# Attention and a gated feed-forward block on one core: the first load of z in rows of four tokens, and a partial-sum copy moved from ScalarE to VectorE

## The chip, the cores and the metric

The kernel runs on one core of a Trainium2 chip. The metric is the device time of one execution in microseconds (us). Before the change the median of six runs is 1193.26 us, from 1192.84 to 1195.26.

## What is computed

The reference, cut to what matters (B = 8 batches, S = 3008 tokens, D = 256, d_qk = 64, d_ff = 2048):

```python
scores = (1.0 / S) * np.matmul(z, z.transpose(0, 2, 1))   # z: [8, 3008, 64]
attn = np.maximum(scores, 0.0) ** 2
x = (u * np.matmul(attn, v)).reshape(B * S, D)            # u, v: [8, 3008, 256]
h = x @ w_in                                              # w_in: [256, 2048]
out = (h * np.cos(h)) @ w_out                             # w_out: [2048, 256]
```

## The kernel before the change, in words

The tokens of a batch are cut into six columns of up to 512 tokens (the last has 448), and each column, one "slot" s of 48, goes through two phases. The first makes the attention output of the column: scores (z times z, line 194), a ReLU on ScalarE that moves them out of PSUM (line 204), a square on VectorE that leaves a piece A in SBUF (lines 209 and 212), and products of the pieces with v that are added up in PSUM (line 258). The second phase takes the column through the feed-forward block: h (line 404), the cosine on ScalarE (line 412), the product g on VectorE (line 415), and the products with w_out (lines 482 and 525). Everything is issued in an order written out by hand, and each engine runs its own list in order.

**The first columns.** Slots 0, 1 and 2 go through `phase_a_first` one after the other, before any whole second phase. Each output half dh (128 of the 256 columns of the output) is added up in two PSUM banks, one for the upper and one for the lower 64 rows of each block of tokens; the two products of a block run side by side on the two halves of TensorE's rows. One half uses the pair of banks M, the other the two banks of one of the E buffers; in slot 1 the roles are swapped. While a slot's products run, the scores of later groups are issued between them into the other E buffers.

**The end of a first column.** At line 379 `gate_sum` is called for both halves. In each, line 269 copies the first bank to an SBUF tile `sm` on ScalarE, and line 270 adds the second bank to it on VectorE. Then `hold` lets GpSimd read one element of the first sum, which keeps the load of the next u (GpSimd's queue) behind it. After slots 1 and 2 units of the second phase follow (their g at line 415 stands behind the sums on VectorE). PSUM banks come free for the next slot when they have been copied or added.

**The start.** z of batch 0 comes in six transfers at lines 633 and 639, issued in turn on SyncE's and ScalarE's queues. Partition p of transfer g receives the tokens p, p+128, p+256 and p+384 of column g: four rows of 64 float32 (256 bytes) that lie 128 tokens apart in memory. A cast (line 645) makes them float16, and four TensorE transposes per column (line 649) put them into PSUM with the four blocks of 128 tokens side by side; `copy_turned` (line 657 on ScalarE for column 0, line 659 on VectorE for columns 1 to 5) copies them to the tile zT, whose column index is the token. Seven matmuls on zeros (line 664) and four more (line 687) keep TensorE busy before and between the first scores.

Of the kernel before, what the change touches and what calls it, by code (L numbers as in the profile page):

```python
# [14 lines left out]
def kernel(  # L15
# [9 lines left out]
    nc = tc.nc  # L25
# [6 lines left out]
    P = 128  # L32
    H = P // 2
    CW = 512
    NB = (S + P - 1) // P
    NC = (S + CW - 1) // CW
# [10 lines left out]
    def width(J):  # L47
        return CW if J < NC - 1 else WL
# [27 lines left out]
    turned = [ppool.tile([P, CW], FP16, name=f"turned{i}", tag=f"M{i % 2}") for i in range(3)]  # L76
# [17 lines left out]
    def drop_piece(key):  # L94
        i = pieces.pop(key)
        if pending.get(i):
            pending[i] = "dropped"
        else:
            free_pieces.append(i)
# [9 lines left out]
    z16s, zTs, vs, u16s, uTs, xs, gs = {}, {}, {}, {}, {}, {}, {}  # L109
# [48 lines left out]
    def turn_u(s):  # L158
        t = upool.tile([P, 8, P], FP16, name="uT")
        nc.sync.dma_start_transpose(t, u16s.pop(s).rearrange("p j d -> p (j d)"))  # L160
        uTs[s] = t
# [20 lines left out]
    def emit_score(later=None):  # L182
        b, J, I, h = groups[done_groups[0]]
        done_groups[0] += 1
        cut = I == J and not (b == 0 and J < 3)
        W = 2 * P if cut and h == 0 else width(J)
        zT = zTs[b]
        e = E[take_e()]
        for t in range(2):
            k = 4 * I + 2 * h + t  # L190
            half = t if h == 0 else 1 - t
            rows = slice(half * H, (half + 1) * H)
            Wt = min(W, (2 * h + t + 1) * P) if cut else W
            nc.tensor.matmul(  # L194
                e[:, t, 0:Wt],
                zT[rows, k * P:(k + 1) * P],
                zT[rows, J * CW:J * CW + Wt],
                start=True,
                stop=True,
            )  # L200
        key = (b, J, I)
        a = new_piece(key) if h == 0 else piece(key)
        r = rpool.tile([P, 2, CW], FP16, name="r")
        nc.scalar.activation(r[:, :, 0:W], e[:, :, 0:W], AF.Relu)  # L204
        def square():
            if I > J:
                a4 = a.rearrange("p (k t j) -> p t k j", k=4, j=P)[:, 2 * h:2 * h + 2, :, :]
                r4 = r.rearrange("p t (k j) -> p t k j", j=P)
                nc.vector.tensor_tensor(a4, r4, r4, ALU.mult)  # L209
            else:  # L210
                a4 = a.rearrange("p (k w) -> p k w", w=CW)[:, 2 * h:2 * h + 2, 0:W]
                nc.vector.tensor_tensor(a4, r[:, :, 0:W], r[:, :, 0:W], ALU.mult)  # L212

        if later is None:
            square()
        else:
            later.append(square)
        if h == 0:
            return
        if cut or (I > J and (b, J, I) not in direct):  # L220
            turns.append(((b, I), key))
            turns.sort(key=lambda t: t[0])
            turn_slots[key] = pieces[key]
            pending[pieces[key]] = "held"

    def emit_turns(due, more=0):
        while turns and (turns[0][0] <= due or more > 0):
            if turns[0][0] > due:
                more -= 1
            (b, c), key = turns.pop(0)  # L230
            b, J, I = key
            i = turn_slots[key]
            a = piece_bufs[i]
            if I == J:
                a4 = a.rearrange("p (k w) -> p k w", w=CW)
                for rr in range(1, 4):
                    rows = P if J * 4 + rr < NB - 1 else H
                    nc.sync.dma_start_transpose(
                        a4[:, 0:rr, rr * P:rr * P + rows],
                        a[0:rows, rr * CW:rr * CW + rr * P],  # L240
                    )
            else:
                d = new_piece((b, I, J))
                nc.sync.dma_start_transpose(d.rearrange("p (n j) -> p n j", j=P), a)
            if pending.pop(i) == "dropped":
                free_pieces.append(i)
# [10 lines left out]
    def emit_value(b, J, k, t, dh, bank, start, stop):  # L257
        nc.tensor.matmul(  # L258
            bank[:, 0:width(J)],
            vs[b, k // 4][t * H:(t + 1) * H, k % 4, dh * P:(dh + 1) * P],  # L260
            value_rhs(b, J, k, t),
            start=start,
            stop=stop,
        )

    def gate_sum(s, b0, b1):
        W = width(s % NC)
        sm = spool.tile([P, CW], FP32, name="sm")
        nc.scalar.copy(sm[:, 0:W], b0[:, 0:W])
        nc.vector.tensor_tensor(sm[:, 0:W], b1[:, 0:W], sm[:, 0:W], ALU.add)  # L270
        return sm

    def gate_mul(s, dh, sm, eng=None):
        eng = eng or nc.vector
        J = s % NC
        b = s // NC
        W = width(J)
        if s not in xs:
            if J == NC - 1 and b % 2 == 1:
                xs[s] = xodd  # L280
            else:
                xs[s] = xpool.tile([P, 2, CW], FP16, name="x")
        x = xs[s]
        uT = uTs[s].rearrange("p (k d) j -> p k d j", d=2)
        nk = W // P
        eng.tensor_tensor(  # L286
            x[:, dh, 0:nk * P].rearrange("p (k j) -> p k j", j=P),
            sm[:, 0:nk * P].rearrange("p (k j) -> p k j", j=P),
            uT[:, 0:nk, dh, :],
            ALU.mult,  # L290
        )
        if nk < 4:
            dst = x[:, dh, nk * P:W] if b % 2 == 1 else xodd[:, dh, W:CW]
            eng.tensor_tensor(
                dst, sm[:, nk * P:W], uT[:, nk, dh, 0:W - nk * P], ALU.mult
            )
# [44 lines left out]
    late_sums = []  # L341
    mix_at = {9: ("s2", 0), 19: ("s2", 1), 29: ("s4", 0), 35: ("s4", 1)}

    def hold(src):
        nc.gpsimd.tensor_copy(mark[:, 0:1], src)

    def phase_a_first(s, n, extra={}):
        b, J = s // NC, s % NC
        ea = e_order.pop(0)
        pair = [E[ea][:, 0, :], E[ea][:, 1, :]]  # L350
        acc = [pair, M] if s == 1 else [M, pair]
        last = NB - 1
        run = 1 if s == 0 else 2
        steps = [
            (dh, k)
            for I in range(0, NC, run)
            for dh in range(2)
            for k in range(4 * I, min(4 * (I + run), last))
        ] + [(2, last)]
        lo, hi = 5 if s == 0 else 2, 42  # L360
        at = {}
        for i in range(n):
            p = lo + (hi - lo) * i // (n - 1)
            at[p] = at.get(p, 0) + 1
        for i, (dh, k) in enumerate(steps):
            if i in extra:
                extra[i]()
            if dh == 2:
                emit_value(b, J, last, 0, 0, acc[0][0], False, True)
                emit_value(b, J, last, 1, 1, acc[1][1], False, True)  # L370
            else:
                for t in range(2):
                    emit_value(
                        b, J, k, t, dh, acc[dh][t], k == 0, k == last - 1 and t != dh
                    )
            if dh > 0 and (k % 4 == 3):
                drop_piece((b, J, k // 4))
                if s > 0:
                    emit_turns((0, 0), 1)
                    if k < 4:  # L380
                        turn_u(s)
                    elif k < 8:
                        for d in range(2):
                            gate_mul(s - 1, d, late_sums.pop(0))
            for _ in range(at.get(i, 0)):
                emit_score(later=squares if s == 0 and i == lo else None)
        if s == 0:
            turn_u(0)
        late_sums.extend(gate_sum(s, *acc[dh]) for dh in range(2))
        hold(late_sums[0][0:1, 0:1])  # L390
        load_u(s + 1)
        e_order.append(ea)
# [237 lines left out]
    for g in range(NC):  # L630
        eng = nc.sync if g % 2 == 0 else nc.scalar
        full = 4 if g < NC - 1 else 3
        eng.dma_start(
            z32[g][:, 0:full, :],
            z[0, g * CW:g * CW + full * P, :].rearrange("(j p) d -> p j d", p=P),
        )
        if full == 3:
            for r in range(2):
                nc.sync.dma_start(z32[g][r * H:(r + 1) * H, 3, :], z[0, S - H:S, :])
# [12 lines left out]
            )  # L652

    def copy_turned(g):
        dst = zTs[0][:, g * CW:(g + 1) * CW]
        if g == 0:
            nc.scalar.copy(dst, turned[g])
        else:
            nc.vector.tensor_copy(dst, turned[g])

    wc = cpool.tile([P, 2, CW], FP16, name="c")
    nc.scalar.activation(wc[:, 0, 0:P], warm[:, 0:P], AF.Sin)
# [118 lines left out]
```

## Time and profile before

| | before |
|---|---|
| median of six runs | 1193.26 us |
| the profiled execution's own time | 1193.04 us |
| its span, first to last instruction | 1191.3 us |
| TensorE busy in the span | 1183.5 us (99%) |
| VectorE busy | 1012.2 us (85%) |
| ScalarE busy | 794.4 us (67%) |
| sum copies on ScalarE, line 269, slots 0 to 2 | 6, of 582 to 606 ns |
| sum adds on VectorE, line 270, slots 0 to 2 | 6, of 681 to 686 ns |
| copy of turned z, column 0, ScalarE, line 657 | 0.585 us |
| copies of turned z, columns 1 to 5, VectorE, line 659 | 0.41 to 0.42 us each |
| the z transfers of 128 KB, issue to landing | 3.7 us median on SyncE's queue, 3.9 on ScalarE's |

The times in the profile are microseconds from the span's start. In a list of instructions by time a line has the start, the length, the engine (PE is TensorE's matmul, DVE VectorE, ACT ScalarE, POOL GpSimd, SP SyncE), the line of the kernel, the operation, and the shapes of output and input. Instructions of one engine overlap by a little, so the distance of two starts is the time that one takes from its engine, and is shorter than its length. The chain of waits follows the work that ended last back to the start: its lines have a start, a length, and the engine and line on which the time was spent.

### The profile page before, as it was taken

The page shows a single profiled execution, that of the slowest core. Times are in us where ns is not written, and L with a number is a line of the kernel's source. Part 1 is how long each engine was busy: PE and PEld are TensorE (multiplying, and loading weights), DVE is VectorE, ACT ScalarE, POOL GpSimd, SP SyncE. Part 2 cuts the span into 40 slices and gives each one's busy share as a digit, 9 for nine tenths or more (in the row PEclk, how much of TensorE's full clock was granted, in tenths as well). Part 3 has the DMA queues.
Part 4 walks back from the last instruction along what each step waited for, and adds up shares of the span by engine and source line. Part 5 has one row for each costly group of instructions (what it writes and reads, how often), then busy time and mean ns, then how long its engine had stood idle before and what let it go on. Part 6 is the DMA issues. An engine that isn't in the chain of part 4 may idle for free.

```text
span 1191.3 us, 29044 instructions
## 1 busy us (share of the span) xinstructions
PE 1183.5 (99%) x11887; PEld 726.3 (61%) x11887; DVE 1012.2 (85%) x1302; ACT 794.4 (67%) x927; POOL 689.1 (58%) x717
## 2 busy tenths in 40 slices
PE   9999999999999999999999999999999999999998
PEld 4566665665566656666566665656666566665566
DVE  6888888889988898888988889888888888888776
ACT  7966676667666676667676676666766666666454
POOL 3286746657466573755647556476565665545452
PEclk9999999999999999999999999999999999999999
DMA  9999998569995699945999459974898839954301
GB/s 160 173 176 156 126 158 131 102 122 139 138 131 97 123 141 162 131 84 104 158 149 131 86 105 162 170 117 71 123 164 148 122 72 126 178 110 86 65 20 54
DMA packets 479862, 148.00 MB, mean 124 GB/s; under 512 B 404208, under 2 KB 479472, under 8 KB 479728
## 3 DMA queue, kind: packets, MB, share of 16 engines
q1 hardware_dynamic: 380752, 112.93, 53.9%
q0 software_dynamic: 97440, 32.78, 26.9%
q8 instruction: 93, 1.52, 0.5%
q10 hardware_dynamic: 1536, 0.43, 0.2%
q14 instruction: 41, 0.34, 0.1%
HBM read 66.32 MB, written 24.64 MB: 76 GB/s over the span
## 4 chain that ended last, share of the span: by engine, by line
PE 97%; ACT 1%; DVE 1%; issue 0%; DMA 0%; POOL 0%; DVEq 0%; ACTq 0%
PE E L404 27%; PE M L482 23%; PE M L258 20%; PE E L258 19%; PE E L194 5%; PE M L525 1%; ACT r L204 1%; PE M L460 1%; DVE g L415 0%; DMA z<-in_z_dram 0%; DVE sm L270 0%; PE E L525 0%; POOL s L433 0%; ACT c L412 0%; DVE A L212 0%
## 5 line engine op out<-in xcount | busy, mean ns | idle before, releaser
L412 ACT ACTIVATE c<-E 128x1024 f16<-128x1024 f32 (+1 forms) x384 | 385.3, 1006 | 216.6 <-PE E L404 214.4
L415 DVE SCALAR_TENSOR_TENSOR g<-E,c 128x1024 f16<-128x1024 f32 (+1 forms) x384 | 458.9, 1197 | 61.6 <-ACT c L412 60.6
L204 ACT ACTIVATE r<-E 128x512 f16<-128x512 f32 (+1 forms) x342 | 327.8, 966 | 112.2 <-PE E L194 106.7
L258 PEld LDWEIGHTS <-v 64*128 64x128 f16 x4512 | 245.3, 94 | 230.0 <-issue 17.5
L404 PE MATMUL E<-x,w_in 128*128 128x512 f16 (+1 forms) x1408 | 354.0, 375 | 0.0
L433 POOL TENSOR_TENSOR s<-g 128x512 f16<-128x512 f16 (+1 forms) x184 | 207.6, 1128 | 189.6 <-DVE g L415 139.6
L258 PE MATMUL M<-A,v 64*128 64x512 f16 (+1 forms) x2256 | 283.0, 372 | 0.0
L258 PE MATMUL E<-A,v 64*128 64x512 f16 (+1 forms) x2256 | 278.0, 372 | 0.0
L434 POOL TENSOR_TENSOR g<-g 128x512 f16<-128x512 f16 (+1 forms) x184 | 218.7, 1188 | 14.4
L404 PEld LDWEIGHTS <-w_in 128*128 128x128 f16 x1536 | 133.1, 98 | 108.9 <-issue 19.5
L482 PEld LDWEIGHTS <-g 128*128 128x128 f16 x2816 | 172.5, 98 | 40.8
L209 DVE TENSOR_TENSOR A<-r 128x1024 f16<-128x1024 f16 x240 | 173.3, 734 | 15.1 <-ACT r L204 14.3
L286 POOL TENSOR_TENSOR x<-sm,uT 128x512 f16<-128x512 f32 (+1 forms) x43 | 48.6, 1131 | 213.6 <-DVE sm L270 213.2
L482 PEld LDWEIGHTS <-s 128*128 128x128 f16 x2112 | 129.4, 98 | 32.1 <-DVE s L440 0.5
L194 PE MATMUL E<-zT 64*128 64x512 f16 (+4 forms) x684 | 127.5, 355 | 1.8 <-DVE sm L270 0.7
L440 DVE TENSOR_TENSOR s<-s,g 128x1024 f16<-128x1024 f16 (+1 forms) x92 | 99.7, 1085 | 2.1 <-POOL s L433 2.1
L482 PE MATMUL M<-w_mix,s 128*128 128x128 f16 x1408 | 94.0, 219 | 0.3 <-POOL s L433 0.3
L482 PE MATMUL M<-w_mix,g 128*128 128x128 f16 x1408 | 93.6, 219 | 0.0
L482 PE MATMUL M<-w_out,g 128*128 128x128 f16 x1408 | 93.6, 219 | 0.0
L212 DVE TENSOR_TENSOR A<-r 128x512 f16<-128x512 f16 (+1 forms) x102 | 80.7, 792 | 8.6 <-ACT r L204 7.9
L194 PEld LDWEIGHTS <-zT 64*128 64x128 f16 x684 | 38.7, 94 | 38.6 <-issue 4.0
L442 DVE TENSOR_TENSOR s<-g,s 128x1024 f16<-128x1024 f16 (+1 forms) x92 | 60.6, 662 | 0.0
(58 smaller groups left out, 647.3 us busy)
## 6 DMA issues: line engine op xcount, KB each, us to landing
out_dram<-o SPq DMA_DIRECT2D x87, 256.0 KB, 2.1
v<-in_v_dram POOLq DMA_DIRECT2D x40, 256.0 KB, 8.8
u<-in_u_dram POOLq DMA_DIRECT2D x40, 256.0 KB, 4.8
A<-A SPq DMA_TRANSPOSE x252, 5.1
z<-in_z_dram POOLq DMA_DIRECT2D x14, 192.0 KB, 10.6
z<-in_z_dram POOLq DMA_DIRECT2D x14, 176.0 KB, 6.0
v<-in_v_dram POOLq DMA_DIRECT2D x8, 192.0 KB, 11.9
u<-in_u_dram POOLq DMA_DIRECT2D x8, 192.0 KB, 3.9
```

Of the source, the lines that this page charges most:

```text
L194: nc.tensor.matmul(e[:, t, 0:Wt], zT[rows, k * P:(k + 1) * P], zT[rows, J * CW:J * CW + Wt], start=True, stop=True,)
L204: nc.scalar.activation(r[:, :, 0:W], e[:, :, 0:W], AF.Relu)
L209: nc.vector.tensor_tensor(a4, r4, r4, ALU.mult)
L212: nc.vector.tensor_tensor(a4, r[:, :, 0:W], r[:, :, 0:W], ALU.mult)
L258: nc.tensor.matmul(bank[:, 0:width(J)], vs[b, k // 4][t * H:(t + 1) * H, k % 4, dh * P:(dh + 1) * P], value_rhs(b, J, k, t), start=start, ...
L404: nc.tensor.matmul(e[:, f, 0:W], w_in16[:, k, ft * P:(ft + 1) * P], x[:, k, 0:W], start=(k == 0), stop=(k == 1),)
L412: nc.scalar.activation(c[:, :, 0:W], e[:, :, 0:W], AF.Sin, bias=half_pi, scale=inv_s2)
L415: return lambda: nc.vector.scalar_tensor_tensor(gs[m][:, 2 * i:2 * i + 2, 0:W], e[:, :, 0:W], 1.0, c[:, :, 0:W], ALU.mult, ALU.mult)
L433: nc.gpsimd.tensor_tensor(s1[:, f, 0:n], g[:, f, low], g[:, lower, low], ALU.add)
L434: nc.gpsimd.tensor_tensor(g[:, f, low], g[:, f, up], g[:, f, low], ALU.subtract)
L440: nc.vector.tensor_tensor(s2[:, f, 0:n], s1[:, f, 0:n], g[:, f, up], ALU.subtract)
L482: nc.tensor.matmul(acc[:, k * P:(k + 1) * P], left[:, ft, k * P:(k + 1) * P], right[:, ft, :], start=(ft == 0 and k == 0), stop=(ft == F - ...
```

## The change

Two things are changed. First, partition p of a z transfer now receives four tokens that follow one another (4p to 4p+3 of the column, 1024 bytes in one piece) for columns 0 to 4; the transposes then leave block j holding the tokens 4p+j, and the copy to zT writes each of its 512 elements four elements apart from the last, which puts the tokens in order again. Column 5, which is not full, is left as it was. Second, in slots 0, 1 and 2 the copy of the first bank for the first half (dh = 0) is done by VectorE instead of ScalarE. The copy of the second half stays on ScalarE, as do all copies of later slots. VectorE's list then has, at the end of each of these slots: the last squares, the copy, the two adds, and (after slots 1 and 2) the products g. The lists of the other engines keep their order, with one copy fewer on ScalarE.

```diff
-    def gate_sum(s, b0, b1):
+    def gate_sum(s, b0, b1, by=None):
         W = width(s % NC)
         sm = spool.tile([P, CW], FP32, name="sm")
-        nc.scalar.copy(sm[:, 0:W], b0[:, 0:W])
+        (by or nc.scalar.copy)(sm[:, 0:W], b0[:, 0:W])
         nc.vector.tensor_tensor(sm[:, 0:W], b1[:, 0:W], sm[:, 0:W], ALU.add)
         return sm
...
-        late_sums.extend(gate_sum(s, *acc[dh]) for dh in range(2))
+        late_sums.extend(
+            gate_sum(s, *acc[dh], by=(nc.vector.tensor_copy, nc.scalar.copy)[dh]) for dh in range(2)
+        )
         hold(late_sums[0][0:1, 0:1])
...
         eng.dma_start(
             z32[g][:, 0:full, :],
-            z[0, g * CW:g * CW + full * P, :].rearrange("(j p) d -> p j d", p=P),
+            z[0, g * CW:g * CW + full * P, :].rearrange(
+                "(p j) d -> p j d" if full == 4 else "(j p) d -> p j d", p=P
+            ),
         )
...
     def copy_turned(g):
-        dst = zTs[0][:, g * CW:(g + 1) * CW]
+        dst, src = zTs[0][:, g * CW:(g + 1) * CW], turned[g]
+        if g < NC - 1:
+            dst = dst.rearrange("q (p j) -> q j p", j=4)
+            src = src.rearrange("q (j p) -> q j p", j=4)
         if g == 0:
-            nc.scalar.copy(dst, turned[g])
+            nc.scalar.copy(dst, src)
         else:
-            nc.vector.tensor_copy(dst, turned[g])
+            nc.vector.tensor_copy(dst, src)
```

## The prediction

> **What bounds the kernel now.** I read the page first (busy time and the shares of the chain), then the busy time by stage, then the chain of waits over the first 60 us, then the single instructions around it. The page's lines on engines and chain:
>
> ```profile
> PE 1183.5 (99%) x11887; PEld 726.3 (61%) x11887; DVE 1012.2 (85%) x1302; ACT 794.4 (67%) x927; POOL 689.1 (58%) x717
> PE 97%; ACT 1%; DVE 1%; issue 0%; DMA 0%; POOL 0%; DVEq 0%; ACTq 0%
> ```
>
> TensorE sets the time. Where it stands idle is seen by stage (length, then busy time and count of PE, PEld, DVE, ACT, POOL):
>
> ```profile
> 5.00:10.00 5.00, 4.56 (x37) 1.88 (x34) 3.96 (x8) 4.36 (x5) 3.58 (x6) 1.00 0.97 132
> 20.00:25.00 5.00, 4.45 (x42) 2.21 (x39) 3.95 (x7) 5.00 (x7) 0.42 (x2) 1.00 1.15 194
> 35.00:40.00 5.00, 4.55 (x30) 1.67 (x28) 4.28 (x7) 4.47 (x6) 1.57 (x3) 1.00 1.18 216
> 50.00:55.00 5.00, 5.00 (x40) 3.02 (x37) 4.10 (x7) 5.00 (x8) 0.18 (x1) 1.00 1.42 190
> 100.00:200.00 100.00, 100.00 (x1016) 59.60 (x1012) 87.31 (x116) 70.10 (x83) 58.81 (x65) 1.00 0.92 138
> ```
>
> All idle time that the change could touch lies before 45 us: at the start, at the end of slot 0 (24 us) and of slot 1 (38 to 41 us). After that TensorE has no gap until the last 41 us, which the change doesn't touch, so a delay or gain in the first 60 us should reach the end unchanged. The chain of waits shows what TensorE waits for:
>
> ```profile
> 0.74 3.19 DMA z<-in_z_dram
> 3.95 0.44 DVE z L645
> 4.43 0.62 PE turned L649 x4
> 5.08 0.59 ACT zT L657
> 5.72 0.41 PE E L194 x2
> ...
> 23.17 0.69 DVE A L212
> 23.86 1.21 DVE sm L270 x2
> 25.11 0.39 PE E L194 x2
> ...
> 37.35 0.40 DVE sm L270
> 37.95 0.68 DVE sm L270
> 38.63 2.37 DVE g L415 x2
> 41.04 0.39 PE E L194 x2
> ```
>
> At both slot ends VectorE is the chain: its last square, two adds, and after slot 1 two products g. ScalarE's copies (line 269) are not on it.
>
> **The sum copies, slot 0.** VectorE's list by time: square at 23.17, add of M at 23.78, add of E at 24.38 (0.68 long, so done at 25.06). The score at 25.11 writes the E buffer that this last add reads. ScalarE's copy of M ran from 23.03 to 23.61, ready before the square was through, so VectorE went from one instruction to the next, 0.60 to 0.61 apart. The change puts one more instruction between the square and the first add. Everything behind it moves by what it takes: the second add, the score, the square at 25.06. ScalarE gets its copy of E 0.47 earlier, but the add of E is now held by VectorE.
>
> What does a VectorE copy of 128x512 float32 from PSUM to SBUF take? No row of before shows it. From below: the copies of turned z (0.42 for 512 float16 from PSUM) and the cast at line 645 (0.43 for 512 float32 from SBUF); less the overlap of 0.08 that the adds show, 0.34. From above: the add of line 270, which also reads 512 float32 from PSUM and writes float32, 0.68 long and 0.60 apart. The other VectorE rows that read float32 from PSUM agree with it on the cost of a column: line 495 takes 0.425 for 256, line 415 takes 1.20 for 1024, and with 0.68 for 512 that is 1.0 ns for each added column. I take the add's **0.60**. Slot 0: +0.60 (bounds +0.34 and +0.60).
>
> The Trainium skill, "VectorE: DVE Perf Modes" (section "Why PSUM operands drop a tier"), says that a PSUM operand leaves VectorE one read port, and float32 from it one element per cycle; its table of cycles gives (120 + 512) / 0.96 GHz = 0.66 us as an estimate. That speaks against moving this copy to VectorE; by it the sum below would be the same within 0.1, while the two-elements rows would make it about half.
>
> **Slot 1.** Here dh = 0 is the E buffer. Square at 36.74, adds at 37.35 and 37.95, then g at 38.63 twice. ScalarE's copy ended at 37.18, so again only VectorE holds the first add. One copy more moves both adds and both g by 0.60. TensorE waits for these: for M's second bank at 38.65, for g at 39.91 and again at 41.04. Between them it has idle time of its own, but each waiting point moves by the same 0.60, so +0.60 (bounds 0.34 and 0.60). ScalarE's cosines come up to 0.1 earlier; their g wait on VectorE anyway.
>
> **Slot 2.** VectorE here:
>
> ```profile
> 53.22 0.69 DVE L209 TENSOR_TENSOR A<-r 128x1024 f16<-128x1024 f16 x1 [0.23 <-ACT r L204]
> 53.82 0.69 DVE L270 TENSOR_TENSOR sm<-M,sm 128x512 f32<-128x512 f32 x1
> 54.42 0.68 DVE L270 TENSOR_TENSOR sm<-E,sm 128x512 f32<-128x512 f32 x1
> 55.11 2.35 DVE L415 SCALAR_TENSOR_TENSOR g<-E,c 128x1024 f16<-128x1024 f32 x2
> ```
>
> TensorE has eight matmuls of line 404 until 54.65 as cover, then line 525 writes M from 54.66; the third of these (0.11 apart, so 54.88) needs M's second bank, which the add freed at 54.51. With the copy it is free at 55.11: 0.23 late, with the semaphore some 0.25. The next unit at 55.53 (then 55.78) needs the E buffer, freed by the second add at 55.70: covered. The g go from 55.11 to 55.71; the E buffers they free are next written at 57.27 and 58.1, by then freed at about 56.9 and 58.1. So **+0.25** (bounds 0, as the cheap copy ends at 54.85, and 0.60, if the g chain binds).
>
> `hold` reads the first sum, which comes 0.60 later; so does the load of the next u on GpSimd's queue and, behind it, the transpose of u and five transposes of A on SyncE's. All of TensorE's work has moved as much, and the transposes issued at 31.35 lie before 50 us and serve slot 3 and later. Cost nothing; without that cover it would be at most the same 0.60.
>
> **The start.** Column 0's way is: landing at 3.95, cast 0.44, transposes at 4.43, copy on ScalarE from 5.08 to 5.66, score at 5.72. TensorE's seven zero matmuls start 0.43 apart from 1.19, so the last ends at 1.19 + 7 x 0.43 = 4.2. If z lands earlier, the transposes can start at 4.2, not before: the gain is at most 0.25. Does it land that much earlier? Between 2.5 and 3.9 us the queues moved 280 to 290 GB/s at 99% busy in rows of 256 bytes. Stores in rows of 1024 bytes landed 1.7 us after issue for 128 KB and 2.1 for 256 KB, against 3.2 for this load; nothing says more than that it lies between no gain and 1.5. A quarter of a us is near the low end, so I take **-0.20** (bounds 0 and -0.25).
>
> The Trainium skill, "DMA: Bandwidth & Descriptors" (section "Why small descriptors are slow"), gives 11 cycles for a 256-byte piece where 8 carry data; four such in one piece would then need some 35 instead of 44, an estimate of 0.2 us less for the 256 KB of the first two columns. No run here shows that yet.
>
> The copies now write every fourth element. Column 0's on ScalarE lies on the chain: no row shows a stepped write; ScalarE takes 1.02 for 1024 columns against 0.585 for 512, 0.85 ns a column; unchanged from below, twice the column cost (+0.44) from above. I take unchanged, being nearest to the row of the same engine. On VectorE 0.42 may become 0.68. Column 1's copy ends at 5.93 and is read at 7.24 (cover 1.3); column 2's delays squares read at 8.79 (cover 0.7); column 3's ends at 9.16 and delays squares read from 11.6; column 4's ends at 10.98, 0.7 before the next VectorE instruction. Cost nothing; without cover 0.26 each. Column 5's copy at 11.71, which TensorE waits for at 12.19, is the old one.
>
> **Sum.** -0.20 + 0.60 + 0.60 + 0.25 = **+1.25 us**. The profiled execution took 1193.04 (span 1191.3 and 1.74 around it), so 1194.29; the median of the runs is 0.22 above it, so 1194.5. That is 0.10%, and about 0.2% (2.4 us) is what a measurement of this kernel can tell from no change.
>
> **Rivals.**
> 1. *The copy is cheap* (0.34): slots give 0.34 + 0.34 + 0, less 0.20 is +0.5, 1193.8. For it: 0.42 rows of VectorE. Against: none of them reads float32 from PSUM.
> 2. *The start gives nothing back*: z lands no earlier and the stepped copy on ScalarE is twice as dear a column: +0.44 + 1.45 = +1.9, 1195.2. For it: no stepped row. A milder form is that TensorE's slow first rate (128-column transposes 0.107 apart until 5.16, full rate at 5.72) catches the earlier scores.
> 3. *TensorE falls back to its slow rate.* At the start matmuls of 512 columns come 0.43 apart, later 0.216, after some 4 us of work. If idle time at the end of slot 1 brings the slow rate back for as long, half of 4.2 us is lost: +2.1 + 1.25 = +3.3, 1196.6, slower by 0.28%. It decides from the point where half idle is enough: between 38.2 and 41.3 TensorE idles about 1.2 us and keeps full rate; the change makes it 1.8 of 3.7. Against: that it holds now at about 40%.
> 4. *ScalarE was the hidden bound*: it loses three copies 0.48 apart, -1.45, with the start -1.65, 1191.6. For it: ScalarE busy 5.00 of 5 at the end of slot 0. Against: the chain, where each add starts as VectorE comes free and not as a copy ends.
>
> **Chances and range.** Forecast 0.56, rival 1 0.16, rival 2 0.13, rival 3 0.07, rival 4 0.08. The unknowns' bounds give 0.68 - 0.25 = +0.4 to 1.8 + 0.44 = +2.2, so 1193.7 to 1195.5; with 0.4 either way for the median (four of the six runs lie within 0.42 of theirs) 1193.3 to 1195.9, which leaves out rivals 3 and 4. Faster by over 0.2% 0.01 (TensorE's idle time from 5 to 45 us is only 1.8), within 0.2% 0.91, slower 0.08 (rival 3 and a little of rival 2).
>
> **What would show it.** In the changed profile: z's first cast before 3.95 and transposes near 4.2; line 657 still near 0.59; a line 269 row on VectorE of 0.66 to 0.69; the score at the start of slot 1 0.4 later (0.60 - 0.20), TensorE's wait at 41.04 about 1.0 later, line 525's first about 1.0 later with a gap after two matmuls. A copy of 0.42 makes it rival 1; 512-column matmuls 0.43 apart near 41 us make it rival 3; a sum that starts earlier than before makes it rival 4.

## The result, and the profile after

The change makes the kernel slower: 1197.26 us median (16 runs) against 1193.28 (36 runs) beside it, 4.0 us more, a ratio of 1.0032 with a 95% interval from 1.0025 to 1.0038. The profiled execution took 1197.02 us, its span is 1195.2. The forecast was +1.25 us, with a range up to 1195.9.

Of the page of the changed kernel, the same two lines that the prediction shows of before:

```profile
PE 1183.8 (99%) x11887; PEld 726.7 (61%) x11887; DVE 1016.8 (85%) x1305; ACT 793.9 (66%) x924; POOL 688.8 (58%) x717
PE 96%; DVE 2%; ACT 1%; issue 1%; POOL 0%; ACTq 0%; DVEq 0%
```

TensorE's work is nearly the same (1183.5 us before), the span is 3.9 longer, so 3.6 us of the loss are idle time of TensorE. VectorE's share of the chain went from 1% to 2%. Busy time by stage (length, then PE, PEld, DVE, ACT, POOL) says where:

```profile
5.00:10.00 5.00, 3.70 (x28) 1.41 (x28) 4.16 (x5) 4.51 (x5) 3.31 (x6) 1.00 0.77 102
10.00:15.00 5.00, 3.46 (x32) 1.54 (x31) 4.46 (x6) 1.64 (x3) 4.26 (x7) 1.00 1.13 138
25.00:30.00 5.00, 3.61 (x36) 1.78 (x33) 3.69 (x7) 3.31 (x5) 0.97 (x2) 1.00 0.69 136
40.00:45.00 5.00, 3.83 (x24) 1.36 (x24) 4.56 (x7) 3.08 (x4) 2.07 (x3) 1.00 1.08 190
100.00:200.00 100.00, 100.00 (x1011) 59.89 (x1011) 86.99 (x116) 69.03 (x82) 58.07 (x63) 1.00 0.93 145
```

Before, the second of these rows was:

```profile
10.00:15.00 5.00, 4.81 (x46) 2.23 (x45) 3.11 (x6) 3.40 (x4) 4.79 (x7) 1.00 0.98 120
```

From 5 to 15 TensorE idles for 2.8 us, against 0.6 before (0.44 and 0.19), where the forecast had a gain. Around the ends of slots 0 and 1, from 20 to 30 and from 35 to 45, it idles for 1.4 and 1.2 us, against 0.7 and 0.5. The chain of waits of the changed kernel names the instructions (start, length, engine, line):

```profile
4.36 0.44 PE turned L653 x4
4.82 1.30 ACT zT L664
...
6.17 0.60 PE E L194 x4
6.78 0.34 PE turned L653 x4
7.14 1.30 DVE zT L666
8.44 1.48 DVE A L212 x2
9.92 1.20 DVE zT L666
11.12 1.11 DVE A L209 x2
12.23 1.22 DVE zT L666
...
14.39 0.41 PE E L194 x2
...
25.37 0.69 DVE A L212
26.06 0.61 DVE sm L269
...
26.70 1.30 DVE sm L270 x2
...
28.04 0.39 PE E L194 x2
```

Column 0's copy on ScalarE now takes 1.29 and not 0.59, and the copies of columns 1 to 4 on VectorE 1.28 to 1.30 and not 0.42. VectorE's copies and squares carry the chain from 7.1 to 13.4; before, only column 5's copy was on it here. Two groups of transposes, those of columns 4 and 5, waited for VectorE's copies (in brackets, TensorE's idle time and what ended it):

```profile
11.17 0.38 PE L653 MATMUL turned_e<-id,z 128*128 128x128 f16 x4 [0.59 <-DVE zT L666]
13.49 0.38 PE L653 MATMUL turned_e<-id,z 128*128 128x128 f16 x4 [0.75 <-DVE zT L666]
```

At the end of slot 0 the new copy (26.06) stands between the square and the two adds, as foreseen.

Four points of the order stand in both profiles, and their shift from before to after splits the loss: the score behind column 5's copy from 12.19 to 14.39 (+2.20); the first score held at the end of slot 0 from 25.11 to 28.04 (+2.93, so 0.73 for this end); the score behind the second g of slot 1 from 41.04 to 44.60 (+3.56, 0.63 for this end); the second unit of line 404 after slot 2 from 55.69 to 59.66 in the chain (+3.97, 0.41 for this end). The lines of before for the first and the last point:

```profile
11.71 0.43 DVE zT L659
12.19 0.41 PE E L194 x2
...
55.69 0.86 PE E L404 x4
```

The lines after for the third and the last point:

```profile
44.60 0.41 PE E L194 x2
...
59.66 0.86 PE E L406 x4
```

Single profiles scatter here: in four other profiles of kernels whose start is that of before, the score that is at 12.19 came at 11.82 to 12.45. So the first of the four parts is known to some 0.3 us.

### The profile page after: what moved, and what is told of

Same layout as the page of the kernel before. It is cut to its first block, busy times and chain, and to the rows that moved or that the text cites. A ratio compares the mean times of both kernels' runs of the same rounds, so it can differ in the third digit from the quotient of the medians.

```text
span 1195.2 us, 29043 instructions
## 1 busy us (share of the span) xinstructions
PE 1183.8 (99%) x11887; PEld 726.7 (61%) x11887; DVE 1016.8 (85%) x1305; ACT 793.9 (66%) x924; POOL 688.8 (58%) x717
## 4 chain that ended last, share of the span: by engine, by line
PE 96%; DVE 2%; ACT 1%; issue 1%; POOL 0%; ACTq 0%; DVEq 0%
PE E L406 27%; PE M L484 23%; PE M L258 20%; PE E L258 19%; PE E L194 5%; ACT r L204 1%; PE M L527 1%; PE M L462 1%; DVE zT L666 0%; DVE g L417 0%; DVE A L212 0%; PE E L671 0%; DVE A L209 0%; DVE sm L270 0%; DVE sm L269 0%
## 5 line engine op out<-in xcount | busy, mean ns | idle before, releaser
L436 POOL TENSOR_TENSOR g<-g 128x512 f16<-128x512 f16 (+1 forms) x184 | 218.7, 1189 | 14.4
L209 DVE TENSOR_TENSOR A<-r 128x1024 f16<-128x1024 f16 x240 | 173.1, 734 | 15.1 <-ACT r L204 14.4
```

Source lines behind the costliest of these rows:

```text
L436: nc.gpsimd.tensor_tensor(g[:, f, low], g[:, f, up], g[:, f, low], ALU.subtract)
```

## The experiments

The theory after the result: the stepped writes make the copies of turned z slow and cost the start 2.2 us; the sum copies cost 1.8 at the three slot ends. Rivals: the sum copies carry most of it; the copies are slow for another reason (the faster loads, or any step in the pattern); part of the loss is a wait for a load. Each run is compared with the kernel before, run beside it.

**The first part alone.** Its edit is the change without its pieces in `gate_sum` and in the call at line 379.

> The first part of the change alone: z in rows of four tokens and the copies that write every fourth element; all six sum copies on ScalarE as before. Theory: the stepped copy takes 1.3 us on either engine (0.585 on ScalarE and 0.42 on VectorE before) and costs the start 2.2 us, so about +2.2 us, 1195.5, with the score of slot 0 that waited at 12.19 coming at 14.4. Rival, that the sum copies carry most of the 4 us: this run within 0.5 us of before.

Measured: 1195.20 us against 1193.65, ratio 1.0015 (1.0006 to 1.0023). The medians differ by 1.55 us, the ratio gives 1.8, somewhat less than the 2.2 expected. The score behind column 5's copy came at 14.11 (expected 14.4), 1.9 later than before, and that shift was still 1.9 to 2.0 in slots 1 and 2. The copies took 1.28 to 1.30. The rival falls.

**The second part alone.**

> The second part alone: the first half's sum copied by VectorE, z loaded and copied as before. Theory: VectorE's copy takes 0.68 and the add behind it does not overlap it, since it reads what the copy wrote, so 0.72 at the ends of slots 0 and 1 and 0.3 to 0.45 at slot 2: +1.5 to +1.9 us, 1194.8 to 1195.2. Rival (the parts are not independent, the late start makes the slot ends dearer): under +1.0 us.

Measured: 1195.41 against 1193.65, ratio 1.0014 (1.0005 to 1.0023): +1.76, as expected, though its profile also has a wait of 0.5 us at line 527 for the load of w_out, so a part of this may be that load. The parts cost about the same.

**Rows of four, not put in order.** The copy stays as it was:

```diff
-            z[0, g * CW:g * CW + full * P, :].rearrange("(j p) d -> p j d", p=P),
+            z[0, g * CW:g * CW + full * P, :].rearrange(
+                "(p j) d -> p j d" if full == 4 else "(j p) d -> p j d", p=P
+            ),
```

> z in rows of four tokens, but plain copies as before and sum copies on ScalarE: it leaves out the putting in order, so the first batch's tokens in zT stand in another order. Theory (the stepped write alone makes the copies slow): copies at 0.585 and 0.42, first cast at 3.6, transposes from 4.15, first score at 5.45, 0.2 to 0.3 us below before: 1193.0. Rival (the faster loads get in the way of the copies): copies near 1.3 us and about +2.2 us, as in the run of the first part alone.

The copies took 0.59 and 0.42, the first cast started at 3.56, the transposes at 4.15, the first score at 5.46, and the score behind column 5's copy at 11.93: the step alone makes the copies slow, not the loads. But the time was 1194.19 against 1193.65, and the ratio of the runs 0.9999 (0.9990 to 1.0008), an interval that holds the quotient of the two medians too: no gain is seen at the end, where 1193.0 was expected. In this profile TensorE waited 1.3 us at line 525 for the load of w_out, a wait that the profile of before doesn't show.

**The order put in by the read.** The copies read PSUM in steps of 256 bytes and write without a gap:

```diff
...
+        if g < NC - 1:
+            dst = dst.rearrange("q (p j) -> q p j", j=4)
+            src = src.rearrange("q (j p) -> q p j", j=4)
...
```

> z in rows of four tokens, put in order by copies that read PSUM in steps of 256 bytes and write zT without a gap; sum copies on ScalarE; the result is the reference's. Theory (what costs is the stepped write to SBUF): ScalarE's copy unchanged at 0.585, VectorE's at most 0.7, so 0.2 to 0.3 us below before, 1193.0. Rival (any step between 2-byte elements costs, in reading too): copies near 1.3 us, about +2.2 us.

ScalarE's copy took 0.59, VectorE's 0.69 and 0.68 (0.42 without a step). The score behind column 5 came at 11.80, 0.39 earlier than before. The median was 1193.41 against 1193.65, ratio 1.0000 (0.9992 to 1.0009), with runs from 1192.48 to 1195.69. The slowest was the profiled one, and TensorE's list of waits in it begins:

```profile
PE M L525 <- DMA w_out<-in_moe_w_out_dram: 2.6, 1, 2.6
```

w_out's load was issued at 38.96 and landed 18.0 later, against 14.4 before, where TensorE needed it 0.9 us after it had landed (39.35 + 14.4 = 53.75, line 525 at 54.66). The load was issued 0.39 earlier than before, as much as the score came earlier, so the earlier start took nothing of this margin; the slower landing used it up (16.7 in the run with rows of four not put in order). Why it landed later is not shown. It needs no faster start: the run with the copies behind the end, further below, is the kernel before up to there, and it waited 0.2 us at line 525 with a landing of 15.7.

**Rows of two**, copies that write every second element.

> z in rows of two tokens (512 bytes), put in order by copies that write every second element; sum copies on ScalarE; the result is the reference's. If each 2-byte element written by itself costs the same whatever lies between: copies near 1.3 us and about +1.5 to 2 us, as with every fourth. Rival, if the cost grows with the distance covered (1024 columns of zT instead of 2048): copies near 0.7 to 0.9 us and under +0.7 us.

Copies of 0.73 to 0.74 on both engines, so the cost of a copy grows with the distance. The time was 1194.47 against 1193.57, ratio 1.0006 (0.9997 to 1.0015): whether it stays under the +0.7 us that was expected for this case can't be told. The profile has a wait of 0.4 us for w_out.

**The cost of the stepped write by itself.** Copies behind the last store's computation:

```diff
+    for eng in (nc.vector.tensor_copy, nc.scalar.copy):
+        for src in (flat[:, 0:CW], E[1][:, 0, :]):
+            for step in (1, 2, 4):
+                eng(wide[:, 0:CW * step].rearrange("p (n s) -> p n s", s=step)[:, :, 0], src)
...
```

> The kernel before with 24 copies appended behind the last store's computation, on VectorE and then on ScalarE: 512 columns of float16 from SBUF and of float32 from PSUM to float16 with one, two and four elements' distance between written elements, then 128 columns of float32 from PSUM to float32 and to float16 with the same distances. Its total time is not compared. If the cost is one of 2-byte elements written alone: the float16 rows rise to about 1.3 us at distance 2 and 4 alike and the float32 rows don't rise. If it is one of the distance in bytes: float16 at distance 4 (8 bytes) is like float32 at distance 2 (8 bytes), and float16 at 2 lies between. If the stepped write only hurts beside the other work of the start: no row rises above 0.75 us.

From PSUM to float16, 512 columns, at distances 1, 2 and 4, VectorE and then ScalarE:

```profile
1183.82 0.69 DVE L756 CAST A<-E 128x512 f16<-128x512 f32 x1
1184.55 0.73 DVE L756 CAST A<-E 128x512 f16<-128x512 f32 x1
1185.32 1.30 DVE L756 CAST A<-E 128x512 f16<-128x512 f32 x1
```

```profile
1193.10 0.59 ACT L756 CAST A<-E 128x512 f16<-128x512 f32 x1
1193.72 0.73 ACT L756 CAST A<-E 128x512 f16<-128x512 f32 x1
1194.48 1.29 ACT L756 CAST A<-E 128x512 f16<-128x512 f32 x1
```

Only the distance of the written elements differs between the rows of one engine, and the engines agree at 2 and 4, so it is the write that decides there. These copies lie at the end of the kernel, so the other work of its start is not to blame. With 128 columns distance 4 took 0.44 on both, so a further column costs (1.30 - 0.44) / 384 = 2.2 ns, and at distance 2 (0.73 - 0.30) / 384 = 1.1 ns. Neither of the two rules that I had written down holds: distances 2 and 4 are not alike, and it is not the distance in bytes, since 128 columns at 8 bytes took 0.44 as float16 and 0.29 (VectorE) as float32. From SBUF, VectorE took 0.28, 0.46 and 0.74, ScalarE 0.62, 0.76 and 1.32. Why VectorE is cheaper from SBUF, and what the mechanism is, stays open.

**An early load of w_out**, on the kernel before and on the one with the stepped read:

```diff
+    nc.gpsimd.dma_start(w_out16, moe_w_out.rearrange("(k p) f -> p k f", p=P))
     phase_a_first(1, 12)
-    nc.gpsimd.dma_start(w_out16, moe_w_out.rearrange("(k p) f -> p k f", p=P))
```

> The kernel before with one change: the load of w_out is issued behind slot 0 instead of slot 1, some 14 us earlier. In the runs with the faster start TensorE waited 1.3 and 2.6 us for this load at line 525. Theory (the load's landing decides the runs above the fastest ones, and takes back what a faster start gains): the wait is gone, the median 0.3 to 0.7 us below before and the runs closer together. Rival (the load, issued earlier, delays u and the transposes): no gain, or a new wait behind a transfer before 60 us.

> Rows of four put in order by stepped reads of PSUM, and w_out's load issued behind slot 0; the result is the reference's. Theory: the start's gain of 0.3 to 0.4 us is no longer lost to the wait for w_out and adds to that of the early load: 0.7 to 1.0 us below before. Rival (something else is late next, a v load or the transposes of u): no better than the early load alone.

The first took 1193.21 (1192.76 to 1193.77) against 1193.57 (1192.80 to 1195.88), ratio 0.9995 (0.9986 to 1.0004); the second 1192.93 (1192.53 to 1193.55), ratio 0.9994 (0.9985 to 1.0003). The issue moved to 25.80 and 25.07, and neither profile has a wait for w_out. The runs lie closer together, as expected, but both gains are within the intervals: a version that beats the kernel before is not shown. Between these two medians the stepped read's start is worth 0.28 us, with runs that overlap.

**The parts once more without the blur of that load.** Column 0 alone with the stepped write (columns 1 to 4 read in steps), then columns 1 to 4 alone. The edit of the first, against the stepped read with the early load:

```diff
-            dst = dst.rearrange("q (p j) -> q p j", j=4)
-            src = src.rearrange("q (j p) -> q p j", j=4)
+            order = "q j p" if g == 0 else "q p j"
+            dst = dst.rearrange("q (p j) -> " + order, j=4)
+            src = src.rearrange("q (j p) -> " + order, j=4)
```

> As the kernel with stepped reads and the early load of w_out (1192.9), but column 0's copy on ScalarE writes every fourth element as in the change; columns 1 to 4 keep the stepped read. Theory (this copy lies on the chain and nothing hides it): +0.7 us, its added length, so 1193.6. Rival (the late copies of VectorE alone carry the loss): within 0.2 us of 1192.9.

The median is 1194.25, 1.3 above 1192.93 and not 0.7 (ratio to the kernel before 1.0007, 0.9998 to 1.0017). But five of the ten runs lie from 1193.22 to 1193.72, five from 1194.79 to 1195.27. The lower five are where the theory put them, +0.6 at their middle (1193.52). The profiled run, 1195.18, is of the upper five, and its chain shows what happened:

```profile
4.36 0.44 PE turned L651 x4
4.82 1.30 ACT zT L663
...
6.17 1.03 PE E L194 x3
7.20 0.54 PE turned L651 x4
```

The transposes at 4.36 are 0.11 apart, TensorE's slow rate. It then idled for 0.96 us behind the copy, and the four score matmuls at 6.17 took 1.03, against 0.61 at 5.72 before: the slow rate was still on, and matmuls came at half speed until about 10 us. The profile's column of granted clock reads 1.00 all the while, so the rate is read from the matmuls' distances alone. The longer idle time does not settle it: in the profiles of the change and of its first part alone TensorE idled the same 0.96 us, and the scores at 6.17 took 0.60; with the early load of w_out alone it idled 0.25, and the scores at 5.59 took 1.03, with the full rate from 6.56. What decides how long the slow rate lasts stays open. That it also made the other four runs of the upper group long is an inference from their times.

> The other way round: column 0 with the stepped read, columns 1 to 4 on VectorE with the stepped write. Theory (two of TensorE's transposes wait for VectorE's copies, 0.6 and 0.75 us in the run of the first part alone, plus 0.1 for a late square): +1.3 to +1.5 us, 1194.2 to 1194.4. Rival (the copies are covered, as the prediction had it): within 0.2 us of 1192.9.

Measured 1194.46 (1194.21 to 1195.22) and ratio 1.0007 (0.9997 to 1.0016) to the kernel before; 1.5 us above 1192.93. Its chain is VectorE from 5.25 to 12.38, and the transposes of columns 4 and 5 waited 0.55 and 0.75 for VectorE's copies, so the prediction's cover did not hold.

> The second part of the change alone, on the kernel with the early load of w_out (1193.2), so that the load's landing doesn't blur it. Theory (0.72 + 0.63 + 0.41 at the three slot ends): +1.6 to +1.9 us, 1194.8 to 1195.1. Rival, the prediction's size: +1.45 us, 1194.7, or less.

Measured 1194.81 (1194.64 to 1195.04), 1.60 above 1193.21; ratio 1.0009 (1.0000 to 1.0018).

> The whole change with the early load of w_out. Theory (the parts add up: 0.7 + 1.4 + 1.75 over the kernel with stepped reads, 1192.9): 1196.6 to 1196.9, no nearer to 1193 than the change itself, since its TensorE work comes after the load anyway. Rival (part of the change's loss is a wait for w_out): 1196.0 or less.

Measured 1196.76 (1196.42 to 1197.32), ratio 1.0028 (1.0018 to 1.0037). It is 3.8 above 1192.93; the parts are 0.6 (lower five), 1.5 and 1.6, together 3.7; with the median of all ten runs for the first they would be 4.4. The change with the late load took 1197.26, so at most some 0.5 us of its 4.0 can be a wait for w_out, and its own profile has none on TensorE's matmuls.

## Why the prediction was wrong, point by point

- *What bounds the kernel, and that a delay in the first 60 us reaches the end*: right. The shift of 3.97 at 59.66 is the span's 3.9.
- *The start, -0.20: z lands earlier and the transposes start near 4.2*: this half was right. The first cast came at 3.58 (3.95 before), the transposes at 4.15, and with plain copies the first score at 5.46, 0.26 earlier. The queues moved up to 392 GB/s in that time, against 280 to 290 before. The landing is shown: the first cast started at 3.45 to 3.58 in all eight profiles with rows of four, at 3.75 to 3.96 in the five with the old rows. The score's 0.26 is less sure, since with the old rows it came between 5.36 and 5.73.
- *"I take unchanged, being nearest to the row of the same engine"* (column 0's copy on ScalarE, +0.44 from above): **this step failed.** It measured 1.29 against 0.585, +0.71, beyond the bound too. The bound was doubled from contiguous copies, while the stepped write has a cost of its own, from PSUM the same on both engines (1.30 and 1.29). No row of the trace had a stepped 2-byte write, and a bound made from rows without the thing in question was no bound.
- *"Cost nothing; without cover 0.26 each"* (columns 1 to 4 on VectorE): **this step failed twice.** The copies grew by 0.88, not 0.26. And the covers were counted only to the scores and values that read the copies; the transposes of columns 4 and 5 wait for the copies of 3 and 4 as well (they lie in one PSUM tile, `turned_e`), 1.3 us in two waits, and squares and copies queue behind each other on VectorE. Alone, with the other parts taken out, this cost 1.5 us. So the start was -0.20 + 0.0 + 0.0 in the forecast and about -0.3 + 0.7 + 1.5 = +1.9 by the runs (+2.2 in the profile after).
- *The sum copies, 0.60 + 0.60 + 0.25 = 1.45*: the mechanism was right, and 1.60 to 1.76 was measured. VectorE's copy is 0.684 long, like the add that it was taken from. Mis-sized is its distance to the add, 0.72 (25.98 to 26.70, and the same at slots 1 and 2) and not 0.60. The add reads what the copy wrote, and the neighbours that are 0.60 to 0.61 apart don't depend on each other; that this is the reason is an inference. At slot 2 line 525's third matmul came 0.3 us late (with the early load of w_out, idle time of 0.25), and 0.1 had gathered since the end of slot 1: 0.41 instead of 0.25. VectorE's two instructions there, of the changed kernel:

```profile
57.38 0.68 DVE L269 COPY sm<-M 128x512 f32<-128x512 f32 x1
58.10 0.69 DVE L270 TENSOR_TENSOR sm<-M,sm 128x512 f32<-128x512 f32 x1
```

- *Rival 1, the cheap copy*: out, 0.684 and not 0.34. *Rival 2, the start gives nothing back and the stepped copy on ScalarE is dear*: the right place, with a price of 1.9 us in total that was too small because VectorE's copies were left out of it. *Rival 3, TensorE falls back*: not at the end of slot 1, where the matmuls of the changed kernel stay at 0.39 to 0.41 a pair. The milder form named under rival 2, the slow rate reaching the scores, is seen in the profiles of two experiments, not in that of the change, whose scores at 6.17 took 0.60. *Rival 4*: out; ScalarE with three copies fewer gave nothing.
- *What hides a gain*: the forecast let the start's gain pass to the end. In both profiles with the gain and the late load of w_out, this load landed 16.7 and 18.0 us after its issue, and TensorE's wait for it took back more than the gain. That is not in the result, as the start lost time.

The Trainium skill, "SBUF — State Buffer" (section "Door 1: The DMA port swizzle"), speaks of 16-byte lines in SBUF and says that a step of up to 8 bfloat16 is free. The runs here disagree for writes of float16, which is as long: 0.59 at distance 1, 0.73 at 2 and 1.29 at 4 on ScalarE; the measurement decides.

## What to carry to other kernels

When a layout is mended by a copy, put the step on the side that is read and keep the write without gaps: here the same reordering cost nothing on ScalarE and 0.26 us a copy on VectorE as a stepped PSUM read, and 0.7 to 0.9 us as a stepped 2-byte write. An operation whose form no row of the trace has is not bounded by doubling a row of another form; measure it, or leave the range open at the top. Count the covers of a slowed copy over everything that waits for it, buffers that are written again included, and over the instructions queued behind it.

## What the runs showed that I had not expected

- A float16 write at a distance of four elements costs 2.2 ns a column on VectorE and ScalarE alike when the source is PSUM (512 columns: 1.30 and 1.29 us); VectorE takes 0.74 for it from SBUF.
- The landing of w_out, 12.3 to 18.0 us after issue in the profiles, sits at the edge of the chain at 54 us. With the load 14 us earlier the slowest of 11 runs was 1193.77; of the 27 runs of before beside them the slowest was 1195.88. How many of the longer runs were this load and how many TensorE's longer slow rate is open; the run of 1193.77, which was profiled, had the slow rate until about 6.5 us and no wait for the load.
- TensorE's slow rate at the start ended at very different times. With the stepped read and the early load eight transposes from 4.11 took 0.61 us, against 1.03 before the change. In the profile before the change the slow rate ended between 5.2 and 5.7 us, with the early load alone at about 6.5, in one profile of column 0's experiment only at about 10 us. The idle time ahead of it doesn't explain this, as said above.
